# Chunked attention feeding a two-layer gated block: another order for a few attention pieces, two accumulators and the Silu pieces

## The chip, the cores and the metric

One core of a Trainium2 chip. The metric is device time in microseconds, from the run's own clock; the median of three runs is given. A separate profiled execution gives the trace. Engines are named as in the profile: PE (TensorE, matmuls), PEld (its weight loads), DVE (VectorE), ACT (ScalarE), POOL (GpSimd, here issuing loads) and SP (SyncE, issuing stores and transposing DMAs).

## The reference

```
q, k, v: [8, 8, 576, 64]            # batch, heads, sequence, head dim
per chunk of 64 positions:  attn = softmax(q_c k_c^T / 8);  out_c = attn v_c
x = out as [4608 tokens, 512]
h = x @ w_in        # [4608, 2048]
g = h * sigmoid(beta * h)
y = g @ w_out       # [4608, 512], fp32
```

## The kernel before, in words

The 4608 tokens are 18 units of 256 tokens; two units make a block of 512, so there are 9 blocks. For each unit the attention is a chain over four engines:

- `T` (`emit_T`): q and k are transposed, by DVE (L164) for units up to 8, by a transposing DMA from SP (L159) for later ones; the call also issues the loads of a later unit on POOL.
- `sc` (`emit_sc`): 64 small matmuls of scores into the PSUM tile `sc`, and the exponential on ACT (L241 or L225).
- `pv` (`emit_pv`): 32 small matmuls (L270, L256) with the values, whose extra column gives the row sums.
- `norm` (`emit_norm`): reciprocal and multiplication on DVE (L307, L313), for each half of a unit.
- the result is transposed into the block's tile `xt`, by PE and an ACT copy (`xp`, `emit_xt_pe`, L329 and L333, units 4 and 5 among others) or by a transposing DMA from SP right after the `norm` (L348, from unit 6 on).

The first layer takes `xt` and `w_in`. In blocks 0 to 5 it is 16 groups `m` per block (`emit_m`): 4 matmuls of 128x512 into a PSUM bank `hps` (L372), a tanh on ACT (L384) and a gate on DVE (L360) that writes 128 rows of `gt` and so frees the bank. From block 6 (`QB`) on, 4 of the 16 groups (0 to 3) are still done so, with a Silu (L381) and a scaling (L356, `mg`). The other 12 are three product groups `q` with 7 products instead of 8 (a Winograd form of Strassen's method). A product group `i` has two PSUM banks, `qx` and `qz`, and runs in four parts (`emit_q`, s = 0 to 3) with products (1, 2), (6, 5), (7, 3) and (4). Between the products ACT copies a bank to `hq` (L503) or DVE adds it (L506); product 5 starts `qz` anew, so it waits until DVE has added product 2 from there. Then come the Silu pieces on ACT (`qs`, L513): piece "2" needs the add of product 7, piece "1" the add of product 3, piece "0" product 4 itself; and the scalings on DVE (`qt`, L527): `qt 0` needs pieces "1", `qt 1` pieces "0" and "2".

The second layer is of the same form for all blocks but block 0: 7 products of 8 matmuls in each of two halves, `prod p,t` (`emit_prod`, L585), 0.87 us per half. Products 1, 6, 7 and 4 go to accumulator 0 and products 2, 5 and 3 to accumulator 1. After each whole product ACT copies the bank to `osb` (L602) or DVE adds it there (L605). Operands of products are sums of `gt`, `sum 0` to `sum 3` on DVE (`emit_sum`, L436, some 1.2 us each), and differences of `w_out`, `wt 0` to `wt 3` (L427). The accumulators of block 1 are two banks of the pool `ps_p` (name `acc`), which has four banks in all, so that the groups of loop 2 have the other two; the accumulators of later blocks are `ya` and `yb`, one bank each. Only block 8 is different at the end: its products 1, 6, 7, 4 go to `acc` banks.

Loop `j` (L738) holds the first layer of block j, the second layer of block j - 1, and attention for block j + 1. The order inside a loop is written out by hand: every piece of work is an item (place between 0 and 1, priority, what), the items are sorted by place and priority (L801), and issued in that order. Every engine has its own queue and takes its instructions in that order. So a number such as `0.36` has no meaning but the order that it gives. `ATT` (L726) gives for each unit the place `a0` and the width `w` over which `att_items` (L719) spreads its chain. `LANE` (L730) is the first layer's order for blocks 6 to 8; there `c`, `e` and `f` are the places of a lane item's start, of the next item and of the one after that.

The start of loop 2 before, as sorted:

```
prod1,0 sum0 sc5 xp4,0 prod1,1 sum1 xp4,1 prod2,0 pv5 norm5,0 norm5,1 prod2,1 T6 sum2 prod6,0
xp5,0 xp5,1 sum3 prod6,1 m0 sc6 wt2 m1 prod5,0 m2 pv6 ... m4 T7 wt3 prod7,0 m5 m6 sc7 T8 T9 prod7,1
m7 m8 pv7 norm7,0 prod3,0 m9 norm7,1 m10 prod3,1 m11 T10 m12 prod4,0 m13 prod4,1 m14 m15
```

Of the kernel before, what the change touches and what calls it, by code (L numbers as in the profile page):

```python
# [8 lines left out]
FP32 = mybir.dt.float32  # L9
# [6 lines left out]
def kernel(  # L16
# [16 lines left out]
    KFF = DFF // 128  # L33
# [21 lines left out]
    ps_y, qs_p, osl_p = [], [], []  # L55
# [22 lines left out]
    NB = len(blocks)  # L78
# [70 lines left out]
    qT = {}  # L149
    kT = {}  # L150
# [260 lines left out]
    def w_at(r, kk, c):  # L411
        g = 2 * r + kk // 4
        return w_out16[g][:, kk % 4, 256 * c:256 * c + 256]
# [134 lines left out]
    def flush_stores():  # L548
        while late:
            emit_store(*late.pop(0))  # L550

    def emit_prod(j, p, t):
        last = j == NB - 1
        if p == 1 and t == 0:
            if j == 1:
                a = [ps_p[0].tile([128, 512], FP32, tag="p", name="acc") for _ in range(2)]
            else:
                a = [ps_y[0].tile([128, 512], FP32, tag=n, name=n) for n in (("yb", "ya") if last else ("ya", "yb"))]
            if last:
                a = [[ps_p[0].tile([128, 512], FP32, tag="p", name="acc") for _ in range(2)], a]  # L560
            acc_t[j] = a
        g = gt_t[j]
        acc = acc_t[j][0 if p in (1, 6, 7, 4) else 1]
        acc, dst = (acc[t][:, 0:256],) * 2 if last else (acc, acc[:, 256 * t:256 * t + 256])
        c0 = t * 128
        for kk in range(8):
            lhsT = {
                1: lambda: g[:, kk, c0:c0 + 128],
                2: lambda: g[:, 8 + kk, c0:c0 + 128],
                3: lambda: sm[3][:, kk, c0:c0 + 128],  # L570
                4: lambda: g[:, 8 + kk, 256 + c0:256 + c0 + 128],
                5: lambda: sm[0][:, kk, c0:c0 + 128],
                6: lambda: sm[1][:, kk, c0:c0 + 128],
                7: lambda: sm[2][:, kk, c0:c0 + 128],
            }[p]()
            rhs = {
                1: lambda: w_at(0, kk, 0),
                2: lambda: w_at(1, kk, 0),
                3: lambda: w_at(1, kk, 1),
                4: lambda: wt[3][:, kk, :],  # L580
                5: lambda: wt[0][:, kk, :],
                6: lambda: wt[1][:, kk, :],
                7: lambda: wt[2][:, kk, :],
            }[p]()
            nc.tensor.matmul(  # L585
                out=dst,
                lhsT=lhsT,
                rhs=rhs,
                start=(p in (1, 2, 5) and kk == 0 and (t == 0 or last)),
                stop=(kk == 7 and (t == 1 or last)),  # L590
                skip_group_check=True,
            )
        if t == 0 and not last:
            return
        flush_stores()
        r, c, how = {1: (0, 0, "copy"), 2: (0, 0, "add"), 6: (0, 1, "copy"), 5: (1, 1, "copy"),
                     7: (1, 1, "add"), 3: (0, 1, "add"), 4: (1, 0, "copy")}[p]
        key = (j, r, c, t if last else None)
        if how == "copy":
            o = osl_p[0].tile([128, 256], FP32, name="osl") if last else osb_p.tile([128, DM], FP32, tag="osb", name="osb")  # L600
            oq_t[key] = o
            nc.scalar.copy(out=o, in_=acc)  # L602
        else:
            o = oq_t[key]
            nc.vector.tensor_tensor(out=o, in0=acc, in1=o, op=ALU.add)  # L605
        if p in (2, 7, 3, 4):
            late.append(key)
# [6 lines left out]
    with tc.manual_schedule():  # L614
# [104 lines left out]
        def att_items(u, a0, w):  # L719
            it = [(a0, 2, ("sc", u)), (a0 + 0.36 * w, 3, ("pv", u)), (a0 + 0.361 * w, 3, ("norm", u, 0)),  # L720
                  (a0 + (0.42 if u >= WV else 0.50) * w, 3, ("norm", u, 1))]
            if u >= WV:
                it.append((a0 + (0.45 * w if u == 9 else 0.005), 3, ("T", u + 3)))
            return it

        ATT = {2: ((6, 0.36, 0.27), (7, 0.60, 0.27)),  # L726
               3: ((8, 0.01, 0.30), (9, 0.28, 0.30), (10, 0.66, 0.33)),
               4: ((11, 0.02, 0.33), (12, 0.35, 0.33), (13, 0.68, 0.33)),
               5: ((14, 0.02, 0.30), (15, 0.30, 0.30), (16, 0.58, 0.30), (17, 0.86, 0.28))}
# [8 lines left out]
        for j in range(1, NB):  # L738
# [6 lines left out]
            items = []  # L745
            if j == 1:
                items += [(0.04 * m, 0, ("h", m)) for m in range(8)]
                items += [(0.32 + 0.0850 * (m - 8), 0, ("m", m)) for m in range(8, KFF)]
                items += [(0.30, 3, ("T", 4)), (0.52, 2, ("sc", 4)), (0.70, 2, ("pv", 4)), (0.71, 3, ("norm", 4, 0)),
                          (0.80, 3, ("norm", 4, 1)), (0.56, 3, ("Th", 5, "kT")), (0.63, 3, ("Th", 5, "qT"))]  # L750
                items += [(c, 3, ("wt", i)) for i, c in ((1, 0.47),)]
            else:
                m0 = {2: 0.36, 4: 0.09}.get(j, 0.02)
                if j < QB:
                    items += [(m0 + (1 - m0) * m / KFF, 0, ("m", m)) for m in range(KFF)]
                else:
                    lane = LANE[2 if j == QB else j == NB - 1]
                    cost = [1 if it[0] == "q" and it[2] == 3 else 2 for it in lane]
                    for n, it in enumerate(lane):
                        c, e, f = (0.98 * sum(cost[:n + d]) / sum(cost) for d in (0, 1, 2))  # L760
                        items.append((c, 0, it))
                        if it[0] == "m":
                            items.append((c + 0.04, 3, ("mg", it[1])))
                        elif it[0] == "last":
                            pass
                        elif it[2] == 2:
                            if j == NB - 1 and it[1] == 3:
                                f = e
                            items += [(f - 0.002, 2, ("qs", it[1], 2)), (f - 0.001, 2, ("qs", it[1], 1)),
                                      (f + 0.03, 3, ("qt", it[1], 0))]  # L770
                        elif it[2] == 3:
                            items += [(c + 0.001, 2, ("qs", it[1], 0)), (c + 0.04, 3, ("qt", it[1], 1))]
                    if j == QB:
                        items.append((0.01, 6, ("open",)))
                        items += [(0.011+0.001*n, 6, ("tx", QB, n)) for n in range(4)]
                    if j + 1 < NB:
                        items += [(0.70 + 0.06 * n, 5, ("tx", j + 1, n)) for n in range(4)]
                for i, p in enumerate((1, 2, 6, 5, 7, 3, 4)):
                    for t in range(2):
                        w = 1.06 if j == NB - 1 else 0.98  # L780
                        items.append(((0.002 if j >= QB else 0) + w * (2 * i + t) / 14, 1, ("prod", p, t)))
                if j == NB - 1:
                    for i, c in ((2, 0.72), (0, 0.80), (1, 0.86)):
                        items.append((c, 4, ("pre", i)))
                for i in range(4):
                    s0 = (0.01, 0.08, 0.25, 0.33)[i] if j == 2 else 0.005 + 0.07 * i
                    if j >= QB:
                        s0 = (0.08, 0.15, 0.33, 0.48)[i] if j == QB else (0.003, 0.10, 0.33, 0.48)[i]
                    items.append((s0, 4, ("sum", i)))
                if j == 2:  # L790
                    items += [(c, 3, ("wt", i)) for i, c in ((2, 0.36), (3, 0.55))]
                    items += [(0.03, 0, ("sc", 5)), (0.06, 2, ("xp", 4, 0)), (0.09, 2, ("xp", 4, 1)),
                              (0.17, 2, ("pv", 5)), (0.18, 3, ("norm", 5, 0)), (0.19, 3, ("norm", 5, 1)),
                              (0.24, 3, ("T", 6)), (0.53, 3, ("T", 7)), (0.60, 3, ("T", 8)), (0.61, 3, ("T", 9)), (0.80, 3, ("T", 10)),
                              (0.30, 2, ("xp", 5, 0)), (0.32, 2, ("xp", 5, 1))]
                for jw, i, c, d in ((3, 2, 0.10, 0.22), (4, 1, 0.21, 0.22), (4, 3, 0.10, 0.22)):
                    if jw == j:
                        items += [(c + d * n, 5, ("ws", i, n)) for n in range(4)]
                for u, a0, w in ATT.get(j, ()):
                    items += att_items(u, a0, w)  # L800
# [54 lines left out]
        for p in (2, 6, 5, 7, 3, 4):  # L855
            for t in range(2):
                emit_prod(NB - 1, p, t)
# [33 lines left out]
```

## Time and profile before

| what | before |
|---|---|
| median of 3 runs | 276.55 us (276.26 to 276.83) |
| the profiled execution, its own time | 276.39 us |
| its span, first to last instruction | 274.6 us |
| granted TensorE clock | 1.00 |
| PE busy | 266.6 us |
| DVE busy | 210.0 us |
| ACT busy | 166.8 us |
| loop 2 starts (`prod 1,0` of block 1) | 62.90 us |
| loop 3 starts (`prod 1,0` of block 2) | 94.83 us |
| last product starts | 269.66 us |

Outside the span lie 276.39 - 274.6 = 1.8 us. Lines of the timeline are: start, duration, engine, line of the kernel, operation, output<-inputs, shapes, count, and in brackets the engine's idle time before it and who ended it. Lines of the chain are: start, duration, what. Lines of the waits are: who waited for whom, total us, times, longest. Matmuls overlap in the records, so that a group of them is shown longer than its distance to the next group.

### The profile page before, as it was taken

Reading aid. Unit: us, or ns where it says so; the run is one execution under the profiler, and the core shown is the slowest. Engines: PE = TensorE matmul, PEld = TensorE weight load, DVE = VectorE, ACT = ScalarE, POOL = GpSimd, SP = SyncE. Lnnn points to the kernel's source line nnn. Section 1 sums busy time; section 2 is a strip of 40 time slices with the busy share of each in tenths; the row PEclk is TensorE's granted clock in tenths of the full one; section 3 lists DMA queues with packets and bytes.
Section 4 is the critical chain, followed back from the end, with each engine's and each line's share of the span. In section 5 each row is a group of like instructions: output and inputs, shape, how many; then the busy total and the mean of one; then the engine's idle time right before and its main releaser. Section 6 shows DMA issues by size and latency. Waiting matters only on the chain.

```text
span 274.6 us, 7824 instructions
## 1 busy us (share of the span) xinstructions
PE 266.6 (97%) x3237; PEld 184.8 (67%) x3237; DVE 210.0 (76%) x394; ACT 166.8 (61%) x300; POOL 95.2 (35%) x122
## 2 busy tenths in 40 slices
PE   7799999999999999999999999999999999999995
PEld 2575445847665666666666666668887887778874
DVE  3567666899998598678977896759896977777961
ACT  2388416976664565556655655576768495858721
POOL 8954478489639935333445200000000000000000
PEclk9999999999999999999999999999999999999999
DMA  9999999999999999999999999853111102110223
GB/s 137 170 195 203 190 181 187 235 171 172 173 149 168 171 174 153 176 146 146 158 153 195 133 137 197 183 147 80 41 54 60 41 0 79 38 41 1 78 79 115
DMA packets 141763, 36.43 MB, mean 133 GB/s; under 512 B 125856, under 2 KB 141216, under 8 KB 141728
## 3 DMA queue, kind: packets, MB, share of 16 engines
q0 software_dynamic: 99136, 18.10, 83.3%
q1 hardware_dynamic: 42592, 17.84, 35.7%
q8 instruction: 25, 0.41, 0.6%
q14 instruction: 10, 0.08, 0.1%
HBM read 36.71 MB, written 9.44 MB: 168 GB/s over the span
## 4 chain that ended last, share of the span: by engine, by line
PE 78%; DVE 10%; ACT 5%; issue 3%; DMA 2%; POOL 0%; DVEq 0%; ACTq 0%; POOLq 0%
PE hps L372 28%; PE ya L585 14%; PE yb L585 11%; PE ops L397 5%; PE acc L585 5%; PE qx L484 4%; PE qz L484 4%; DVE gt L360 3%; ACT hq L513 3%; DMA sm<-in_k_dram 2%; DVE gt L527 2%; PE sc L232 2%; DVE sm L436 1%; PE sc L219 1%; PE x L270 1%
## 5 line engine op out<-in xcount | busy, mean ns | idle before, releaser
L372 PE MATMUL hps<-xt,win 128*128 128x512 f16 (+1 forms) x488 | 106.5, 355 | 0.5 <-DVE gt L360 0.3
L384 ACT ACTIVATE sg<-hps,bt 128x512 f32<-128x512 f32 (+1 forms) x111 | 69.3, 635 | 35.0 <-PE hps L372 32.6
L360 DVE SCALAR_TENSOR_TENSOR gt<-sg,hps 128x512 f16<-128x512 f32 (+1 forms) x111 | 67.6, 617 | 27.7 <-ACT sg L384 26.8
L372 PEld LDWEIGHTS <-win 128*128 128x128 f16 x488 | 46.2, 98 | 32.1 <-issue 1.0
L585 PEld LDWEIGHTS <-sm 128*128 128x128 f16 x512 | 49.4, 98 | 12.0 <-issue 0.3
L585 PEld LDWEIGHTS <-gt 128*128 128x128 f16 x384 | 36.9, 98 | 10.3 <-DVE gt L527 0.8
L120 POOL DMA_DIRECT2D vbig<-in_v_dram x40 | 34.0, 864 | 24.8 <-DMA ku<-in_k_dram 7.4
L585 PE MATMUL ya<-wt,sm 128*128 128x256 f16 x200 | 25.9, 273 | 0.0
L527 DVE TENSOR_SCALAR gt<-hq,rb 128x512 f16<-128x512 f32 x36 | 16.3, 483 | 8.4 <-ACT hq L513 7.2
L106 POOL DMA_DIRECT2D qu<-in_q_dram x20 | 17.1, 872 | 14.1 <-DVE qT L164 5.8
L106 POOL DMA_DIRECT2D ku<-in_k_dram x20 | 17.1, 880 | 12.2 <-DMA qu<-in_q_dram 7.8
L513 ACT ACTIVATE hq<-hq,bs 128x256 f32<-128x256 f32 (+1 forms) x36 | 19.2, 612 | 1.8 <-DVE hq L506 1.8
L436 DVE TENSOR_TENSOR sm<-gt 128x2048 f16<-128x2048 f16 (+1 forms) x17 | 19.7, 1156 | 0.3
L602 ACT COPY osb<-ya 128x512 f32<-128x512 f32 x18 | 10.6, 589 | 8.6 <-PE ya L585 7.9
L484 PEld LDWEIGHTS <-ws 128*128 128x128 f16 x144 | 14.1, 98 | 2.4 <-issue 0.7
L241 ACT ACTIVATE et<-sc 128x1024 f16<-128x1024 f32 (+1 forms) x10 | 8.3, 852 | 11.4 <-PE sc L232 11.4
L397 PE MATMUL ops<-wout,gt 128*128 128x512 f16 x64 | 14.7, 379 | 0.0
L585 PE MATMUL yb<-wout,gt 128*128 128x256 f16 x104 | 13.9, 273 | 0.3 <-DVE gt L527 0.2
L585 PE MATMUL yb<-wt,sm 128*128 128x256 f16 x104 | 13.5, 273 | 0.1
L503 ACT COPY hq<-qx 128x512 f32<-128x512 f32 x18 | 10.6, 587 | 4.9 <-PE qx L484 4.8
L585 PE MATMUL ya<-wout,gt 128*128 128x256 f16 x104 | 13.5, 273 | 0.0
L585 PE MATMUL yb<-wout,sm 128*128 128x256 f16 x104 | 13.5, 273 | 0.0
(99 smaller groups left out, 355.7 us busy)
## 6 DMA issues: line engine op xcount, KB each, us to landing
out_dram<-osb SPq DMA_DIRECT2D x32, 256.0 KB, 2.8
vbig<-in_v_dram POOLq DMA_DIRECT2D x32, 128.0 KB, 7.5
qu<-in_q_dram POOLq DMA_DIRECT2D x18, 128.0 KB, 12.5
ku<-in_k_dram POOLq DMA_DIRECT2D x18, 128.0 KB, 14.6
win<-in_moe_w_in_dram POOLq DMA_DIRECT2D x8, 256.0 KB, 8.7
wout<-in_moe_w_out_dram POOLq DMA_DIRECT2D x4, 512.0 KB, 13.2
qu<-in_q_dram POOLq DMA_DIRECT2D x5, 256.0 KB, 7.0
ku<-in_k_dram POOLq DMA_DIRECT2D x5, 256.0 KB, 7.1
```

Source lines behind the costliest of these rows:

```text
L106: nc.gpsimd.dma_start(out=tv[off:off + n, sp], in_=src[b, :, s:s + n, :].rearrange("h p d -> p h d"),)
L120: nc.gpsimd.dma_start(out=vbig[off:off + n, i % NV, :, 0:D], in_=v[b, :, s:s + n, :].rearrange("h p d -> p h d"),)
L360: nc.vector.scalar_tensor_tensor(out=gt_t[j][:, m, c0:c0 + n], in0=sg[:, 0:n], scalar=1.0, in1=hps[:, 0:n], op0=ALU.add, op1=ALU.mult,)
L372: nc.tensor.matmul(out=hps[:, 0:n], lhsT=w_in16[m // 2][:, kk, (m % 2) * 128:(m % 2) * 128 + 128], rhs=xr[:, c0 // CH:(c0 + n) // CH, 2 * ...
L384: nc.scalar.activation(out=sg[:, 0:n], in_=hps[:, 0:n], func=ACTF.Tanh, scale=bt[:, m:m + 1])
L397: nc.tensor.matmul(out=ops, lhsT=gt_t[j][:, kk, t * 128:(t + 1) * 128], rhs=w_out16[kk // 4][:, kk % 4, :], start=(kk == 0), stop=(kk == K ...
L436: nc.vector.tensor_tensor(out=sm[i][:, lo:hi, :], in0=a, in1=b, op=op)
L484: nc.tensor.matmul(out=dst[:, s, :], lhsT=lhsT, rhs=rhs, start=(p in (1, 2, 5) and s == 0 and kk == 0), stop=(s == 1 and kk == 1), skip_gr ...
L503: nc.scalar.copy(out=o, in_=z if p == 5 else x)
L513: nc.scalar.activation(out=o, in_=src, func=ACTF.Silu, scale=bs[:, m:m + 1])
L527: nc.vector.tensor_scalar(out=gt_t[j][:, m, :], in0=hq[:, b].rearrange("p c q -> p (c q)"), scalar1=rb[:, m:m + 1], scalar2=None, op0=ALU. ...
L585: nc.tensor.matmul(out=dst, lhsT=lhsT, rhs=rhs, start=(p in (1, 2, 5) and kk == 0 and (t == 0 or last)), stop=(kk == 7 and (t == 1 or last ...
```

## The change

Four parts; no operation is added or taken away.

1. Loop 2, first part: the scores of unit 5 come after `prod 1,1` instead of before it, `xp 4,0` with them; `T 6` comes a place later in the sorted list without passing anything on DVE; `sum 2` and `sum 3` come later, so that on DVE `sum 3` now stands behind the gate of group 0 and behind `wt 2`. (The changed numbers of loop 1 leave its sorted order as it was.)
2. Loop 2, second part: unit 6 a little later and unit 7 over a wider stretch: `pv 7` and `norm 7,0` after `prod 3,0`, and `norm 7,1` after group 10.
3. `ya` and `yb` by turns: accumulator 0 is `yb` in even blocks and `ya` in odd ones. Block 8 is as before.
4. Loops 6 to 8: pieces "2" of each product group come one lane item earlier, and pieces "1" and `qt 0` of product group 3 too, which was so in loop 8 already.

The start of loop 2 as it is then sorted:

```
prod1,0 sum0 prod1,1 sc5 xp4,0 sum1 xp4,1 prod2,0 pv5 norm5,0 norm5,1 prod2,1 T6 prod6,0 sum2
xp5,0 xp5,1 prod6,1 m0 wt2 sum3 sc6 m1 prod5,0 m2 pv6 ... m4 T7 wt3 prod7,0 m5 m6 sc7 T8 T9 prod7,1
m7 m8 prod3,0 pv7 norm7,0 m9 m10 norm7,1 prod3,1 m11 T10 m12 prod4,0 m13 prod4,1 m14 m15
```

The end of loops 6 and 7 (block 6; `tx` are four short differences on DVE):

```
before: prod3,1 mg2 q3,2 tx2 prod4,0 m3 tx3 prod4,1 mg3 qs3,2 qs3,1 q3,3 qs3,0 qt3,0 qt3,1
after:  prod3,1 mg2 q3,2 tx2 prod4,0 qs3,2 qs3,1 m3 tx3 qt3,0 prod4,1 mg3 q3,3 qs3,0 qt3,1
```

```diff
@@ emit_prod
             else:
-                a = [ps_y[0].tile([128, 512], FP32, tag=n, name=n) for n in (("yb", "ya") if last else ("ya", "yb"))]
+                a = [ps_y[0].tile([128, 512], FP32, tag=n, name=n) for n in (("ya", "yb") if j % 2 else ("yb", "ya"))]
@@ ATT
-        ATT = {2: ((6, 0.36, 0.27), (7, 0.60, 0.27)),
+        ATT = {2: ((6, 0.38, 0.27), (7, 0.60, 0.33)),
@@ items of loop 1
-                items += [(0.32 + 0.0850 * (m - 8), 0, ("m", m)) for m in range(8, KFF)]
-                items += [(0.30, 3, ("T", 4)), (0.52, 2, ("sc", 4)), (0.70, 2, ("pv", 4)), (0.71, 3, ("norm", 4, 0)),
-                          (0.80, 3, ("norm", 4, 1)), (0.56, 3, ("Th", 5, "kT")), (0.63, 3, ("Th", 5, "qT"))]
+                items += [(0.32 + 0.0820 * (m - 8), 0, ("m", m)) for m in range(8, KFF)]
+                items += [(0.30, 3, ("T", 4)), (0.49, 2, ("sc", 4)), (0.70, 2, ("pv", 4)), (0.71, 3, ("norm", 4, 0)),
+                          (0.80, 3, ("norm", 4, 1)), (0.56, 3, ("Th", 5, "kT")), (0.61, 3, ("Th", 5, "qT"))]
@@ items of the lanes
                         elif it[2] == 2:
-                            if j == NB - 1 and it[1] == 3:
+                            if it[1] == 3:
                                 f = e
-                            items += [(f - 0.002, 2, ("qs", it[1], 2)), (f - 0.001, 2, ("qs", it[1], 1)),
+                            items += [(e - 0.002, 2, ("qs", it[1], 2)), (f - 0.001, 2, ("qs", it[1], 1)),
                                       (f + 0.03, 3, ("qt", it[1], 0))]
@@ sums and loop 2
-                    s0 = (0.01, 0.08, 0.25, 0.33)[i] if j == 2 else 0.005 + 0.07 * i
+                    s0 = (0.01, 0.08, 0.28, 0.36)[i] if j == 2 else 0.005 + 0.07 * i
...
-                    items += [(0.03, 0, ("sc", 5)), (0.06, 2, ("xp", 4, 0)), (0.09, 2, ("xp", 4, 1)),
+                    items += [(0.07, 2, ("sc", 5)), (0.08, 2, ("xp", 4, 0)), (0.12, 2, ("xp", 4, 1)),
                               (0.17, 2, ("pv", 5)), (0.18, 3, ("norm", 5, 0)), (0.19, 3, ("norm", 5, 1)),
-                              (0.24, 3, ("T", 6)), (0.53, 3, ("T", 7)), (0.60, 3, ("T", 8)), (0.61, 3, ("T", 9)), (0.80, 3, ("T", 10)),
+                              (0.27, 3, ("T", 6)), (0.53, 3, ("T", 7)), (0.60, 3, ("T", 8)), (0.61, 3, ("T", 9)), (0.80, 3, ("T", 10)),
                               (0.30, 2, ("xp", 5, 0)), (0.32, 2, ("xp", 5, 1))]
```

## The prediction

> **What bounds the kernel now.** I read the busy row first, then who waited for whom on PE, then the chain that ended last, then the timeline around each place that the change touches.
>
> ```profile
> PE 266.6 (97%) x3237; PEld 184.8 (67%) x3237; DVE 210.0 (76%) x394; ACT 166.8 (61%) x300; POOL 95.2 (35%) x122
> ```
>
> ```profile
> PE qz L484 <- DVE hq L506: 0.4, 2, 0.2
> PE hps L372 <- DVE gt L360: 0.3, 1, 0.3
> PE sc L232 <- DVE x L313: 0.3, 1, 0.3
> PE yb L585 <- DVE gt L527: 0.2, 1, 0.2
> ```
>
> PE is busy for 97% of the span, and the change takes no matmul away and adds none. So it can only gain by closing waits of PE or by shortening the tail. "Busy" includes modelled ends, so I measured waits as the start of one matmul to the start of the next, less the usual pitch of its shape (a 128x512 matmul 0.216 us, a 128x256 one 0.109). After 40 us this leaves these gaps: 0.43 before the scores of unit 5 (64.20), 0.28 before the scores of unit 7 (81.06), 0.50 before group 12 of block 2 (89.64), 0.34 twice inside a first-layer product (213.74 and 238.93), and 0.39, 0.29 and 0.27 in the tail (260.99, 261.38, 264.43). A change of operation costs 0.09 to 0.12 by itself, in both kernels.
>
> The gap at 89.64, in the timeline:
>
> ```profile
> 87.60 0.69 ACT L384 ACTIVATE sg<-hps,bt 128x512 f32<-128x512 f32 x1 [0.17 <-PE hps L372]
> ...
> 88.06 0.20 DVE L307 RECIPROCAL rd<-x 128x8 f32<-128x8 f32 x1
> 88.30 0.69 DVE L313 TENSOR_TENSOR x<-x,rd 128x512 f16<-128x512 f32 x1
> 88.91 0.68 DVE L360 SCALAR_TENSOR_TENSOR gt<-sg,hps 128x512 f16<-128x512 f32 x1
> ...
> 89.64 1.02 PE L372 MATMUL hps<-xt,win 128*128 128x512 f16 x4 [0.34 <-DVE gt L360]
> ```
>
> In loop 2 two of the four ps_p banks are held by acc, so a first-layer group needs the bank of the group two before it. Group 12 waits for the gate of group 10 (88.91 to 89.59), and that gate stood behind the normalisation of unit 7 (88.06 to 88.99), though its tanh had ended at 88.29. The gap at 213.74 is seen in the chain:
>
> ```profile
> 207.50 0.59 ACT osb L602
> 208.09 0.73 ACT hq L513 x2
> 208.82 0.59 issue
> 209.41 0.72 ACT hq L513
> 210.15 1.29 DVE gt L527 x3
> 211.50 1.11 issue
> 212.61 0.48 DVE gt L356
> 213.09 0.61 DVE hq L506
> 213.74 0.60 PE qz L484 x4
> ```
>
> The Silu pieces of product group 3 end late on ACT, the DVE scalings and sum 0 (211.47 to 212.70) follow, and the add that empties qz comes behind them all. PE waits for that add.
>
> **Part 1: unit 5 half a product later.** After `prod 1,0` (62.90, 0.87 us) PE goes straight into `prod 1,1`, so it reaches the scores at 64.73, and the normalisation that they need has ended (63.46 + 0.69 = 64.15). The gap of 0.43 goes. What is late next: DVE has no idle time here.
>
> ```profile
> 66.63 1.23 DVE L436 TENSOR_TENSOR sm<-sm,gt 128x2048 f16<-128x2048 f16 x1
> ...
> 68.62 0.20 DVE L307 RECIPROCAL rd<-x 128x8 f32<-128x8 f32 x1
> 68.85 0.69 DVE L313 TENSOR_TENSOR x<-x,rd 128x512 f16<-128x512 f32 x1
> ...
> 69.28 0.72 PE L329 MATMUL xp<-ident,x 128*128 128x128 f16 x8
> ```
>
> The second four of these transposes start at 69.60, 0.06 after DVE's 69.54. DVE's list up to there is the same in the changed kernel, so PE comes earlier and waits there instead: gain 0.00 up to 69.60. Behind it sum 3 (1.22) moves past the gate of group 0 and past `wt 2`. Gate 0 then starts at 72.49 rather than 73.50; gate 1 follows wt 2 (pitch 0.60) and sum 3 (1.13) and ends at 72.49 + 0.60 + 0.60 + 1.13 + 0.68 = 75.50, rather than 75.38. Group 3, which needs its bank, starts at 75.55 against 75.57. I take 0.00; from the rows the ends are a gain of the whole 0.43 and a loss of 0.2 (gate 1 a little later than counted). The gap at 81.06 stays: the tanh of group 4, its gate and the two transposes (79.71 to 81.01) keep their order.
>
> **Part 2: units 6 and 7 spread.** `pv 7` after `prod 3,0` moves PE work about (0.38 past 0.87) and DVE is still busy with gate 8 until 85.93, so it costs nothing. The gate of group 10 now stands ahead of the normalisation 7,1: it starts when its tanh is done, 88.32, and ends at 89.00, and group 12 starts at 89.14, 0.50 earlier. What is late next: reciprocal and normalisation (0.85), the add of `prod 3` (0.60) and then gate 11, which ends at 88.32 + 0.60 + 0.85 + 0.60 + 0.68 = 91.05. Group 13 needs that bank and would otherwise start at 89.14 + 0.86 + 0.87 = 90.87; it starts at 91.10, against 91.37 before. Gates 12 to 15 then keep up. Gain 0.27, between 0 and 0.50. The DMAs: the transpose that brings the second half of unit 7 into `xt` is issued by SP at 89.88 rather than 89.02. One store and the two transposes of unit 10 are behind it on SP's queue, and scores 10 come only late in loop 3. POOL's queue of loads keeps its order.
>
> **Part 3: ya and yb by turns.** Between two blocks PE shows no gap over 0.125 us beyond the pitch (100 to 187 us), so now it gains nothing: 0.00, at most 0.1 at each of five boundaries. But it covers part 4: there the copy out of the last product of block 5 comes at 208.35 to 208.95, and PE starts product 1 of block 6 at 208.60. In the same bank PE would wait 0.4; in the other one, last read at 204.02 to 204.71, it doesn't.
>
> **Part 4: Silu pieces earlier.** ACT in loop 6, from rows: the adds of DVE end at 205.70 and 206.30 as before; pieces "2" run 205.75 to 206.45 (0.37 each), pieces "1" to 207.87 (0.69 each), the Silu of group 3 to 208.49, the copy to 208.95, pieces "0" (0.41 each) to 209.70. Before, they ended at 210.84. On DVE the last two scalings end at 210.23 instead of 211.43, sum 0 at 211.5 instead of 212.70, and the add that empties qz at 212.45 instead of 213.68. PE needs qz at 213.40. The gap of 0.34 goes, with 0.95 to spare, and the same at 238.93: 0.68 together, between 0 and 0.69. The Silu of group 3 now waits behind pieces that wait for DVE, from 206.69 to 207.80; behind it are the copy above and, on PE, group 1 of the next block at 211.22, so 2.7 us of cover.
>
> The Trainium skill ("PSUM — Partial Sum Buffer", Engine vs sequencer instructions) says that the queues of ScalarE and VectorE are strictly first in, first out, which speaks against a piece put early that waits for DVE. The trace agrees (ACT stood idle for 1.85 us before the pieces at 257.65, though later copies were to come); it is the third rival.
>
> In the tail pieces "2" of group 2 move ahead of a copy, so pieces "1" end 0.8 us earlier than 253.84, and the second scaling of 253.26 (1.10 for the two, where 0.95 is usual) no longer waits. From there DVE runs without a break to 264.03 and sets the last products: 0.15, between 0 and the 0.95 of all tail gaps.
>
> **Sum.** 0.00 + 0.27 + 0.00 + 0.68 + 0.15 = 1.10 us. The profiled execution took 276.39 (span 274.6), so 275.29; the median of the runs is 276.55, 0.16 above it, so I predict **275.4**, between the two scales. A measurement of this kernel can tell about 0.2% (0.55 us) from no change.
>
> **Rivals.**
> 1. Slower: the transpose of unit 7 lands late. Issued at 89.88, it must land before group 0 of block 3, at 96.49 - 0.27 = 96.22, so it has 6.3 us; the three of this stretch took 4.9 to 6.0 (the one in question 6.0). The larger ones of `kT` just behind took 8.4. With 8.4, PE waits 2.1 us there: 275.4 + 2.1 = 277.5. It outweighs the gains from a landing of 7.4 us on. Against it: a store issued at 90.26 took 5.9. By the Trainium skill ("DMA: Bandwidth & Descriptors", Anatomy of one DMA — SWDGE (gpsimd) path) a DMA has a fixed cost of about 2 us; by that this rival could not be, but the rows show three times as much, and they decide. Chance 0.08.
> 2. The gain of part 1 holds, because DVE also gets ahead: 274.9. Against it: no idle DVE between 64 and 73 us. Chance 0.10.
> 3. ACT, held by pieces that wait for DVE, passes the wait on to PE: the 0.68 stays away, 276.1, no change. For it: the strict order of ACT; against it, 2.7 us of cover. Chance 0.10.
> 4. The change doesn't do what it says: every closed gap reopens at the next DVE result, as in part 1, and the tail sets the end: 276.4. DVE is busy for 76% of the span, yet idle for 0.4 to 1.7 us at several places in loops 6 to 8. Chance 0.10.
>
> The forecast itself, 275.1 to 275.8, has 0.55; 0.07 is left for mixtures, some of them slower. Faster by over 0.2%: 0.55 + 0.10 + some of the mixtures and of rival 3 = 0.72. Within: 0.18. Slower: rival 1 and a mixture, 0.10. The range reaches from rival 2, with a little more tail, to rivals 3 and 4: 274.7 to 276.6.
>
> **What would show it.** Right: no gap before qz of product 5 in loops 7 and 8; the add that empties qz ends about a microsecond before PE needs it; group 12 of block 2 without a gap and 0.2 left at group 13; a new wait at the second transpose of unit 5 where the scores of unit 5 waited. Wrong: PE waiting for a DMA at the first group of loop 3; a wait of ya or yb for an ACT copy at the start of a block; loop 3 (94.83 before) starting over 0.5 us earlier, or later.

## The result, and the profile after

The kernel after takes **275.79 us** (median of 7 runs, 275.34 to 276.16), the kernel before 276.83 in runs beside it (median of 7, 276.26 to 277.81). The ratio is 0.9965, 95% interval 0.9953 to 0.9977: 1.0 us or 0.35% faster. The forecast was 275.4 against a median of 276.55, a gain of 1.15. The profiled execution of after took 276.16, its span is 274.4, and its clock 1.00.

The busy row of after:

```profile
PE 266.0 (97%) x3237; PEld 184.9 (67%) x3237; DVE 209.7 (76%) x394; ACT 167.5 (61%) x300; POOL 95.4 (35%) x122
```

PE has the same number of instructions and the same share as before, so this row alone does not show the gain. Who waited for whom on PE, in the window from 64 to 272 us:

```profile
PE xp L329 <- DVE x L313: 0.3, 1, 0.3
```

All four waits shown of before have gone (`qz`, the groups of loop 2, the scores, the tail's `yb`). One is new, and it is the one that part 1 was expected to make. Waits shorter than a matmul's modelled end are not in this view; one of those matters below.

The span is only 0.2 us shorter, though the median fell by 1.0. The two profiled executions differ before the change bites: loop 2 starts at 62.90 in before and at 63.89 in after, 1.0 us later, and in the experiments it started anywhere from 62.5 to 64.3, while the order of all work ahead of it is the same. So I compare starts on PE measured from the start of loop 2 (negative is earlier than before, us; the experiments in the lower rows are described below):

| kernel | `prod 6` of block 1 | loop 3 | loop 7 | loop 8 | last product | loop 2 at |
|---|---|---|---|---|---|---|
| after | -0.33 | -0.53 | -0.51 | -0.75 | -1.22 | 63.89 |
| p1_only | -0.33 | -0.03 | -0.03 | -0.04 | -0.04 | 62.52 |
| p2_only | 0.00 | -0.50 | -0.50 | -0.50 | -0.51 | 63.36 |
| p34_only | -0.01 | -0.01 | 0.00 | -0.23 | -0.71 | 63.09 |
| gate_first | -0.33 | -0.52 | -0.49 | -0.83 | -1.41 | 64.27 |
| gate_first_again | -0.33 | -0.52 | -0.52 | -0.86 | -1.44 | 63.30 |
| no_swap | -0.33 | -0.52 | -0.15 | -0.13 | -0.71 | 63.66 |
| hold_bank | -0.33 | -0.30 | -0.30 | -0.54 | -1.01 | 63.58 |
| more | -0.33 | -0.87 | -0.87 | -1.21 | -1.78 | 63.90 |
| short_before_2 | 0.00 | -0.07 | -0.07 | -0.08 | -0.31 | 63.12 |
| short_p1_2 | -0.33 | -0.24 | -0.24 | -0.24 | -0.48 | 62.84 |

From the start of loop 2, after is 1.22 us faster: 0.53 in loop 2, 0.24 in loop 7 and 0.47 in loop 8 with the tail. The starts agree within 0.03 us between two executions of one kernel (gate_first and gate_first_again), so they separate what timings with intervals of about 0.2% can't.

The stretch of the old 0.50 gap, in after's timeline (lines of PE, DVE and ACT):

```profile
88.42 0.69 DVE L360 SCALAR_TENSOR_TENSOR gt<-sg,hps 128x512 f16<-128x512 f32 x1 [0.69 <-ACT sg L384]
88.56 0.69 ACT L384 ACTIVATE sg<-hps,bt 128x512 f32<-128x512 f32 x1 [0.17 <-PE hps L372]
89.23 1.89 PE L372 MATMUL hps<-xt,win 128*128 128x512 f16 x8
89.28 0.69 DVE L360 SCALAR_TENSOR_TENSOR gt<-sg,hps 128x512 f16<-128x512 f32 x1 [0.17 <-ACT sg L384]
89.88 0.20 DVE L307 RECIPROCAL rd<-x 128x8 f32<-128x8 f32 x1
90.12 0.69 DVE L313 TENSOR_TENSOR x<-x,rd 128x512 f16<-128x512 f32 x1
90.73 0.68 DVE L605 TENSOR_TENSOR osb<-acc,osb 128x512 f32<-128x512 f32 x1
90.96 1.04 PE L585 MATMUL acc<-wt,gt 128*128 128x256 f16 x8
91.33 1.27 DVE L360 SCALAR_TENSOR_TENSOR gt<-sg,hps 128x512 f16<-128x512 f32 x2
91.83 1.03 PE L372 MATMUL hps<-xt,win 128*128 128x512 f16 x4
```

The gate of group 10 (89.28) follows its tanh at once; the normalisation stands behind it, at 90.12. PE runs groups 11 and 12 without a break (89.23, 8 matmuls). And group 13 starts at 91.83, while the gate of group 11, the first of the two that begin at 91.33, ends only at about 92.0. That is not what the prediction said, and is the first thing to explain.

The boundary of blocks 5 and 6 in after:

```profile
206.22 2.13 ACT L513 ACTIVATE hq<-hq,bs 128x256 f32<-128x256 f32 x4 [1.84 <-DVE hq L506]
...
208.25 0.67 ACT L381 ACTIVATE sg<-hps,bs 128x512 f32<-128x512 f32 x1
208.82 0.57 ACT L602 COPY osb<-ya 128x512 f32<-128x512 f32 x1
...
208.96 0.49 DVE L356 TENSOR_SCALAR gt<-sg,rb 128x512 f16<-128x512 f32 x1
209.08 1.14 PE L585 MATMUL yb<-wout,gt 128*128 128x256 f16 x8
...
212.25 0.68 DVE L506 TENSOR_TENSOR hq<-qz,hq 128x512 f32<-128x512 f32 x1
...
213.98 0.60 PE L484 MATMUL qz<-tx,ws 128*128 128x256 f16 x4
```

The add that empties `qz` ends at 212.93, 1.05 us before PE uses `qz` (213.98). But product 1 at 209.08 is recorded at 1.14 where its kind takes 1.04, and the Silu of group 3 (208.25) stands behind four pieces. The second thing to explain is this 0.10.

### The profile page after: what moved, and what is told of

The parts are those of the page before. It is cut to its first block, busy times and chain, and to the rows that moved or that the text cites. A ratio compares the mean times of both kernels' runs of the same rounds, so it can differ in the third digit from the quotient of the medians.

```text
span 274.4 us, 7822 instructions
## 1 busy us (share of the span) xinstructions
PE 266.0 (97%) x3237; PEld 184.9 (67%) x3237; DVE 209.7 (76%) x394; ACT 167.5 (61%) x300; POOL 95.4 (35%) x122
## 4 chain that ended last, share of the span: by engine, by line
PE 67%; DMA 14%; DVE 10%; POOL 5%; issue 2%; ACT 2%; DVEq 0%; POOLq 0%
PE hps L372 23%; PE ya L585 14%; PE yb L585 14%; PE qx L484 5%; DMA wout<-in_moe_w_out_dram 5%; PE qz L484 4%; PE acc L585 4%; DMA qu<-in_q_dram 3%; DMA win<-in_moe_w_in_dram 3%; DMA ku<-in_k_dram 3%; DVE sm L436 3%; DVE gt L360 2%; POOL vbig L120 2%; PE sc L219 1%; POOL qu L112 1%
## 5 line engine op out<-in xcount | busy, mean ns | idle before, releaser
L513 ACT ACTIVATE hq<-hq,bs 128x256 f32<-128x256 f32 (+1 forms) x36 | 19.9, 610 | 5.5 <-DVE hq L506 5.5
L585 PE MATMUL yb<-wt,sm 128*128 128x256 f16 x152 | 19.7, 273 | 0.1
L585 PE MATMUL ya<-wt,sm 128*128 128x256 f16 x152 | 19.7, 273 | 0.0
L506 DVE TENSOR_TENSOR hq<-qz,hq 128x512 f32<-128x512 f32 x18 | 12.3, 683 | 1.1 <-ACT hq L503 0.8
L278 DVE TENSOR_TENSOR x<-x,rx 128x512 f16<-128x512 f32 (+1 forms) x20 | 11.9, 620 | 0.3
```

The costliest lines, as they stand in the source:

```text
L506: nc.vector.tensor_tensor(out=o, in0=x if p == 7 else z, in1=o, op=ALU.add)
L513: nc.scalar.activation(out=o, in_=src, func=ACTF.Silu, scale=bs[:, m:m + 1])
L585: nc.tensor.matmul(out=dst, lhsT=lhsT, rhs=rhs, start=(p in (1, 2, 5) and kk == 0 and (t == 0 or last)), stop=(kk == 7 and (t == 1 or last ...
```

## The experiments

**Theory**: the gain is 0.5 us in loop 2 by part 2 alone, 0.5 by part 4 (with part 3 as its condition) and 0.2 in the tail; part 1 only moves a wait. **Rivals**: part 1 holds a gain; part 3 gains by itself or isn't needed; the early pieces cost nothing.

### One part at a time: p1_only, p2_only, p34_only

p1_only is before with part 1's places alone, p2_only is before with the wider stretch of unit 7 alone

```diff
-        ATT = {2: ((6, 0.36, 0.27), (7, 0.60, 0.27)),
+        ATT = {2: ((6, 0.36, 0.27), (7, 0.60, 0.33)),
```

and p34_only with the changed line of `emit_prod` and the two changed lines of the lanes.

> Part 1 alone (scores of unit 5 a half product later, transposes of unit 6, sums 2 and 3 and scores 6 moved as in the change). Theory: DVE sets the second transpose of unit 5, so the gap of 0.43 before the scores of unit 5 goes and one of about 0.42 comes before that transpose; loop 3 starts at the same distance from the start of loop 2, within 0.05 us; ratio 1.000. Rival (DVE gets ahead too): 0.4 us faster, ratio 0.9985, no new gap at the transpose.

> Part 2 alone (unit 7 spread wider: pv 7 after product 3,0, the normalisation 7,1 after group 10). Theory after the result: the whole gap of 0.50 before group 12 of block 2 goes and none comes back at group 13, because the bank of accumulator 1 is free by then; loop 3 starts 0.49 us earlier after the start of loop 2; ratio 0.998. Rival (the prediction's sum): 0.2 us comes back at group 13, 0.27 us remain, ratio 0.999.

> Parts 3 and 4 alone (ya and yb by turns, Silu pieces earlier), loop 2 as before. Theory: the two gaps of 0.34 before qz of product 5 go, two gaps of 0.10 come inside product 1 of blocks 6 and 7 (it reads the rows that the scaling of group 3 writes, which now comes later), the tail is 0.24 shorter; together 0.34 x 2 - 0.10 x 2 + 0.24 = 0.72 us, ratio 0.9974. Rival (the wait is only passed on to ACT and DVE): nothing, 1.000.

Measured: p1_only 276.59 (11 runs), ratio 0.9997 (0.9988 to 1.0006); p2_only 276.36 (12 runs), 0.9987 (0.9978 to 0.9996); p34_only 275.87 (5 runs), 0.9967 (0.9955 to 0.9979), beside 276.82 (23 runs of before). By the starts the parts are worth 0.04, 0.51 and 0.71, together 1.26 against 1.22 of the whole: they add up, so no part takes from another.

Where part 1's 0.33 goes is seen in p1_only:

```profile
68.46 0.69 DVE L313 TENSOR_TENSOR x<-x,rd 128x512 f16<-128x512 f32 x1
68.56 0.39 PE L329 MATMUL xp<-ident,x 128*128 128x128 f16 x4
...
69.21 0.40 PE L329 MATMUL xp<-ident,x 128*128 128x128 f16 x4 [0.26 <-DVE x L313]
```

PE reaches the first four transposes earlier than before, and the second four wait for the multiplication that ends at 69.15; they start 0.06 behind it. The gap of 0.43 ahead of the scores of unit 5 has become one of 0.42 here.

### Is DVE the cause of that wait? short_before, short_p1 and a second pair

If DVE's list ahead of that multiplication sets it, half of `sum 1` taken away (1.22 to 0.69) must let part 1 gain. Both kernels of a pair leave out half of `sum 1`; a copy on ACT fills the operand that it would have written, so that no memory is read unwritten:

```diff
-                    emit_sum(j - 1, it[1])
+                    emit_sum(j - 1, it[1], 0, 4 if j == 2 and it[1] == 1 else 8)
...
+                    nc.scalar.copy(out=sm[1][:, 4:8, :], in_=gt_t[0][:, 0:4, 0:256])
```

> Before, with sum 1 of block 1 over half of its rows only (the other half of that tile is filled by an ACT copy in loop 1, so product 6 of block 1 works on other numbers): takes some 0.55 us off DVE right ahead of the normalisation of unit 5. Theory: the gap of 0.43 before the scores of unit 5 stays, since it lies ahead of sum 1; loop 3 starts up to 0.2 us earlier than in before.

> Part 1 alone with the same shorter sum 1 (half of its rows left out, as in short_before). Theory (DVE took back what part 1 gained): with DVE 0.55 us earlier the gap of 0.42 at the second transpose of unit 5 closes, and part 1 is now worth about 0.3 us (loop 3 starts that much earlier after the start of loop 2 than in short_before), where it is worth 0.03 with the full sum. Rival (something other than DVE's list held PE there, ACT's copies or the banks): the gap stays and part 1 is worth 0.03 again.

Measured, one execution each: 277.08 and 276.61. Inconclusive: the copy stood in loop 1 and delayed tanhs there, so that DVE entered loop 2 late and the gap ahead of the scores of unit 5 grew from 0.43 to 0.91. The second pair has the same copy in loop 0.

> As short_before (half of the rows of sum 1 of block 1 left out, so product 6 of block 1 works on other numbers), but the filling ACT copy stands in loop 0, where ACT has nothing to do, instead of loop 1, where it delayed the tanhs and with them DVE. Theory: the gap of 0.42 before the scores of unit 5 is there as in before; loop 3 up to 0.2 us earlier after the start of loop 2 than in before.

> Part 1 alone with the same shorter sum 1 and the filling copy in loop 0. Theory (DVE took back what part 1 gained): DVE is 0.55 us earlier at the normalisation of unit 5, so the gap of 0.42 at its second transpose closes and part 1 is worth about 0.3 us against short_before_2. Rival (ACT's copies or the banks held PE): the gap stays, part 1 is worth 0.03.

Measured, one execution each: 276.30 and 275.86. Loop 3 starts at -0.07 and -0.24, so part 1 is worth 0.17 there, against 0.03 with the whole sum. In short_p1_2:

```profile
66.57 0.69 DVE L436 TENSOR_TENSOR sm<-sm,gt 128x1024 f16<-128x1024 f16 x1
...
68.25 0.69 DVE L313 TENSOR_TENSOR x<-x,rd 128x512 f16<-128x512 f32 x1
...
68.89 0.61 PE L329 MATMUL xp<-ident,x 128*128 128x128 f16 x8
...
73.42 1.22 DVE L436 TENSOR_TENSOR sm<-gt,sm 128x2048 f16<-128x2048 f16 x1
...
74.56 0.68 DVE L360 SCALAR_TENSOR_TENSOR gt<-sg,hps 128x512 f16<-128x512 f32 x1
...
75.29 1.02 PE L372 MATMUL hps<-xt,win 128*128 128x512 f16 x4
```

All eight transposes run as one group of 8 at 68.89, and the gap is closed: DVE was the cause. But less than the 0.3 that I expected stays. Up to group 3 the kernel keeps its 0.33 over short_before_2; there PE waits for the gate of group 1 (74.56 to 75.24), which stands behind `sum 3`. The gap ahead of group 3 is 0.28, in short_before_2 it is 0.12, the change of operation alone. (Group 0 waits for ACT's copies of the transposes, a gap of 0.23, but it does so in both kernels.) The mechanism stands; the size of my expectation was wrong, by the next wait.

### Why group 13 didn't wait: hold_bank

In p2_only and after, the 0.23 that the prediction kept for group 13 isn't there. Theory: when product 3 has been added (90.73 to 91.41 in after), accumulator 1 of block 1 is through, and its bank goes back to the pool of four, so group 13 has a third bank and needs no gate. The experiment holds the bank by one more read of it, on DVE after the products:

```diff
+                    items.append((0.955, 6, ("hold",)))
...
+                elif it[0] == "hold":
+                    nc.vector.tensor_copy(out=braw[:, 0:1], in_=acc_t[1][1][:, 0:1])
```

> The changed kernel with one DVE copy of a single column from the bank of accumulator 1 after gate 14 of loop 2, into a tile that nothing reads any more; the bank is so kept from the groups until then. Theory: in the changed kernel group 13 did not wait for gate 11, since the accumulator's bank had become free as a third one; with the bank held, group 13 waits for gate 11, a gap of about 0.2 us, and loop 3 starts 0.30 rather than 0.53 us earlier after the start of loop 2 than before. Rival (gate 11 was simply early enough, whatever the banks): no gap at group 13, 0.5 us.

Measured, one execution: 276.09; loop 3 starts at -0.30 where after has -0.53.

```profile
90.42 0.68 DVE L605 TENSOR_TENSOR osb<-acc,osb 128x512 f32<-128x512 f32 x1
...
90.65 1.04 PE L585 MATMUL acc<-wt,gt 128*128 128x256 f16 x8
...
91.01 1.27 DVE L360 SCALAR_TENSOR_TENSOR gt<-sg,hps 128x512 f16<-128x512 f32 x2
...
91.74 1.02 PE L372 MATMUL hps<-xt,win 128*128 128x512 f16 x4
```

Group 13 starts 1.09 after the product's start instead of 0.87, a gap of 0.22, just behind the gate of group 11 (91.01 plus half of 1.27 is 91.65). So the bank is the cause, and the prediction's 0.23 was right for a kernel that keeps it.

### Does part 4 need part 3? no_swap

After, with `emit_prod`'s line as it was before:

```diff
-                a = [ps_y[0].tile([128, 512], FP32, tag=n, name=n) for n in (("ya", "yb") if j % 2 else ("yb", "ya"))]
+                a = [ps_y[0].tile([128, 512], FP32, tag=n, name=n) for n in (("yb", "ya") if last else ("ya", "yb"))]
```

> The changed kernel without part 3 (ya and yb in the order of before). Theory: part 3 covers part 4. At the starts of loops 7 and 8 product 1 writes the bank that ACT still copies product 4 from; that copy ended 0.31 us after the start of product 1 in the changed kernel (209.39 against 209.08), so PE waits 0.36 there; the gap of 0.10 inside product 1 is hidden by it. 0.26 us a place, 0.52 us slower than the changed kernel, 0.7 us faster than before. Rival (the banks don't matter): as the changed kernel, 1.21 us faster than before from the start of loop 2 on.

Measured: 275.95 (7 runs) beside 276.63 (10), ratio 0.9978 (0.9966 to 0.9989). By the starts -0.71 instead of -1.22: 0.51 lost, in two waits of 0.37 and 0.36 less the two of 0.10 (next experiment), which they cover.

```profile
208.59 0.57 ACT L602 COPY osb<-ya 128x512 f32<-128x512 f32 x1
...
209.21 1.03 PE L585 MATMUL ya<-wout,gt 128*128 128x256 f16 x8 [0.20 <-ACT osb L602]
```

Product 1 of block 6 starts 0.05 after the copy out of the same bank ends (209.16). Part 3 is needed, for what part 4 does. That part 3 alone gains nothing was not run.

### The 0.10 in product 1: gate_first

Product 1 reads `gt` of group 3 by its fourth matmul. That matmul starts at 209.50 in after, 0.09 late, just behind the scaling that ends at 209.45, which waited for a Silu behind the pieces. gate_first is after with pieces "1" behind that Silu again, and only pieces "2" ahead of it:

```diff
-                            if it[1] == 3:
+                            if j == NB - 1 and it[1] == 3:
```

> The changed kernel, but in loops 6 and 7 the Silu pieces that need product 3 (pieces 1 of group 3) and the first scaling come behind the Silu of group 3 again, only pieces 2 stay ahead. Theory: the scaling of group 3 is back before product 1 of the next block begins, so the two gaps of 0.10 inside product 1 go, and the add that empties qz still ends before PE needs it (about 0.4 us to spare): 0.2 us faster than the changed kernel, 1.43 us (ratio 0.9948) against before. Rival (the 0.10 is not that scaling, or the pieces are needed earlier): the 0.10 stays or the gap before qz of product 5 returns in part: no faster than the changed kernel, ratio 0.9955 or more.

> gate_first once more beside it on the same chip: 1.42 us from the start of loop 2 to the end against before, as in its first profile; ratio 0.995 to 0.996.

Measured: 275.62 (5 runs) beside 276.82, ratio 0.9961 (0.9947 to 0.9974); and again 275.33 (12 runs) beside 276.87, 0.9940 (0.9921 to 0.9960).

```profile
206.62 0.91 ACT L513 ACTIVATE hq<-hq,bs 128x256 f32<-128x256 f32 x2 [1.85 <-DVE hq L506]
...
207.57 0.69 ACT L381 ACTIVATE sg<-hps,bs 128x512 f32<-128x512 f32 x1
...
208.29 0.49 DVE L356 TENSOR_SCALAR gt<-sg,rb 128x512 f16<-128x512 f32 x1 [0.44 <-ACT sg L381]
...
209.48 1.04 PE L585 MATMUL yb<-wout,gt 128*128 128x256 f16 x8
...
213.08 0.68 DVE L506 TENSOR_TENSOR hq<-qz,hq 128x512 f32<-128x512 f32 x1
...
214.27 0.60 PE L484 MATMUL qz<-tx,ws 128*128 128x256 f16 x4
```

The scaling of group 3 ends 0.7 before product 1 begins, the product is back at 1.04, and the add of `qz` still ends 0.51 before its use. The last product starts at -1.41 and -1.44 instead of -1.22: the two of 0.10 are the cost of pieces "1", which don't have to be so early.

### The gaps that part 1 and unit 7 leave: more

more is gate_first with `sum 3` behind the gate of group 1, and the scores of unit 7 behind `prod 7,1`:

```diff
-                    s0 = (0.01, 0.08, 0.28, 0.36)[i] if j == 2 else 0.005 + 0.07 * i
+                    s0 = (0.01, 0.08, 0.28, 0.425)[i] if j == 2 else 0.005 + 0.07 * i
...
-            it = [(a0, 2, ("sc", u)), (a0 + 0.36 * w, 3, ("pv", u)), (a0 + 0.361 * w, 3, ("norm", u, 0)),
+            it = [(a0 + (0.035 if u == 7 else 0), 2, ("sc", u)), (a0 + 0.36 * w, 3, ("pv", u)), (a0 + 0.361 * w, 3, ("norm", u, 0)),
```

> gate_first with two more moves in loop 2: sum 3 of block 1 behind gate 1 (it stood ahead of it), and the scores of unit 7 one half product later, behind product 7,1. Theory: the gap of 0.30 before group 3 shrinks to 0.1 or less and the gap of 0.28 before the scores of unit 7 goes, each as a wait for DVE's list, and nothing takes them back; loop 3 starts about 1.0 us earlier after the start of loop 2 than in before (0.52 in gate_first); about 0.45 us faster than gate_first, ratio 0.994 to 0.995 against before. Rival (as with part 1, the next DVE result gives the wait back): 0.1 us or less over gate_first.

Measured: the gaps of 0.30 at group 3 and 0.28 ahead of the scores of unit 7 have shrunk to 0.12 and 0.09. Loop 3 starts at -0.87, 0.35 earlier than in gate_first and not 0.5, because what is left of them is the change of operation, which stays. The last product starts at -1.78. Time 275.41 (12 runs) beside 276.87, ratio 0.9947 (0.9923 to 0.9972); gate_first in the same runs has 0.9940. The trace shows 0.35 more, the times can't tell the two apart. Both are faster than before; whether either is faster than after is shown by the starts alone, since the intervals overlap with after's.

## Why the prediction was right, step by step

The forecast was a gain of 1.10, and from loop 2 on the trace shows 1.22. Three of its terms were off: part 2 by +0.23, the tail by +0.09 and part 4 by -0.20. That their sum comes so close is in part luck.

- **Part 1, 0.00**: right, 0.03 to 0.04. The wait moved to the second transpose of unit 5, 0.06 behind DVE as foreseen, and gate 1, late behind `sum 3`, took most of the rest at group 3. Rival 2 fell: DVE has nothing to give there, and where it had (short_p1_2), the next wait took half of it.
- **Part 2, 0.27**: right in mechanism, too small; 0.50. The step that failed is "Group 13 needs that bank". It took the bank of accumulator 1, freed by the add of product 3 (hold_bank). The prediction counted the banks at the start of the stretch, not when each comes free.
- **Part 3, 0.00 and cover for part 4**: the cover is shown. Without it PE waits 0.37 and 0.36 (the prediction: 0.4).
- **Part 4, 0.68**: too large; 0.48. Both gaps at `qz` went, with 1.05 to spare (0.95 foreseen). The step that failed is "behind it are the copy above and, on PE, group 1 of the next block at 211.22, so 2.7 us of cover". Of the Silu of group 3 it took only the bank into account and not the reader of its result: the scaling, and through it the fourth matmul of product 1. This is rival 3 in small, 0.10 twice. By the Trainium skill ("PSUM — Partial Sum Buffer", Engine vs sequencer instructions) the queues of ACT and DVE are strictly first in, first out; the trace agrees, with the Silu at 208.25 right behind the four pieces in after, and at 207.57 behind two in gate_first.
- **Tail, 0.15**: 0.24, but that part 4 is the cause is not shown. In after DVE's list there no longer breaks at the second scaling, as the prediction said:

```profile
251.44 1.34 ACT L513 ACTIVATE hq<-hq,bs 128x512 f32<-128x512 f32 x2
...
253.26 0.87 DVE L527 TENSOR_SCALAR gt<-hq,rb 128x512 f16<-128x512 f32 x2
...
254.05 1.22 DVE L436 TENSOR_TENSOR sm<-gt 128x2048 f16<-128x2048 f16 x1
```

Pieces "1" end at 252.78 and the two scalings take 0.87 instead of 1.10; the sum starts at 254.05, with loop 2 a full microsecond later than in before. The first tail gap shrank from 0.39 to 0.23. But short_before_2 and short_p1_2, which have neither part 3 nor part 4, gain the same 0.24 between loop 3 and the last product (see the table), and their first tail gap is 0.23 as well. What sets the kernels with the shorter tail apart is the start of an ACT copy ahead of these pieces. First before, then short_before_2:

```profile
250.26 0.60 PE L484 MATMUL qx<-xt,win 128*128 128x256 f16 x4
251.23 0.59 ACT L503 COPY hq<-qx 128x512 f32<-128x512 f32 x1 [1.06 <-PE qx L484]
...
253.26 1.10 DVE L527 TENSOR_SCALAR gt<-hq,rb 128x512 f16<-128x512 f32 x2
```

```profile
250.40 0.60 PE L484 MATMUL qx<-xt,win 128*128 128x256 f16 x4
251.09 0.58 ACT L503 COPY hq<-qx 128x512 f32<-128x512 f32 x1 [0.79 <-PE qx L484]
...
253.39 0.88 DVE L527 TENSOR_SCALAR gt<-hq,rb 128x512 f16<-128x512 f32 x2
```

In before, p1_only and p2_only the copy starts 0.97 after the first of the four matmuls that it reads; in every other kernel it is 0.69 or 0.70, and in these alone the tail is shorter. With the copy on time the scalings don't wait even with the pieces in their old order. With the pieces earlier by the prediction's 0.8 they would not wait behind a late copy either, but no kernel here has that. Why the copy is late in three kernels is open. Only the 0.48 at `qz` is therefore shown to be the gain of part 4.

- **Rival 1** (the transpose of unit 7 lands late) didn't come. In after it is issued at 90.84 and lands at 96.21, 5.4 us, and the first group of block 3 starts at 96.97 without a wait. The 2 us that the prediction set against this rival are given by the Trainium skill ("DMA: Bandwidth & Descriptors", Anatomy of one DMA — SWDGE (gpsimd) path) for DMAs issued by GpSimd; this one is issued by SP, and the trace's 5.4 us decide.
- **Rival 4** (all gaps reopen) held for part 1 alone.
- **The scale**: the sum was set against medians. The median of before was 276.55 in three runs and 276.83 in seven; by that alone, 0.3 of the difference to the forecast is not the change's.

Still open: why loop 2 starts up to 1.8 us apart. Most of it lies ahead of the first group of the first layer, which starts at 13.4 us in p1_only, 13.8 in before, 14.6 in after and 15.0 in gate_first; from there to loop 2 the executions differ by 0.4 at most. In after PE waits for loads there:

```profile
PE hps L372 <- DMA win<-in_moe_w_in_dram: 0.7, 2, 0.5
```

These two are after's only waits of PE on a load of `w_in`; before and p1_only have none. But gate_first has none either and starts later still, and no run here holds the loads apart.

## What to carry to other kernels

When an item is moved ahead of another on an in-order engine, follow the delayed one to every reader of its result, not only to the bank that it frees: here the cover was said to be 2.7 us and was less than nothing for one reader. Before counting a wait for a buffer, list when each buffer of the pool comes free, accumulators too. And a wait that a lagging engine causes is not closed by moving its consumer: ask which result of that engine is needed next. Last, before a gain is put down to a part of the change, look for it in the traces of the experiments that leave this part out: here that is how the tail lost its explanation.

## What the runs showed of the hardware

- Executions of kernels whose order is the same up to loop 2 reach it at 62.5 to 64.3 us. This is larger than the whole effect of the change; starts measured from loop 2 on repeat to 0.03 us.
- PE starts 0.05 to 0.06 us after the end of the DVE or ACT instruction that it waits for (69.15 to 69.21 in p1_only, 209.16 to 209.21 in no_swap).
- A change from the large matmuls to the small attention ones costs 0.09 us, and back 0.12, also where nothing waits.
- A wait of 0.1 us in the middle of a product shows in no list of waits of PE; it is seen in the recorded length (1.14 instead of 1.04) and in the start of its fourth matmul.
